# Batch 0 of an attention-and-routing kernel: eight rows of q ahead of v, key sums in two banks, the third range's query products amid the first quotient, and a 64-key remainder as 128 zero-padded rows

## The chip, the cores and the metric

The kernel runs on one core of one Trainium2 chip. The metric is the device time of one execution in microseconds (us). The engines are TensorE (PE in the profile; PEld is its weight load), VectorE (DVE), ScalarE (ACT), GpSimd (POOL) and SyncE (SP), which here only issues transfers.

## The reference

Two blocks in a row. The first is an attention without softmax, for 4 batches, 4 heads, 1088 positions and 32 values per head; the second sends its output through eight experts that are weighted by a Sinkhorn iteration.

```
phi(x) = outer product of S1 x and S2 x          # 8 x 8 = 64 features per position
kv  = sum over s of phi(k)[s] * v[s]             # 64 x 32 per head
z   = sum over s of phi(k)[s]                    # 64 per head
x   = (phi(q) . kv) / (phi(q) . z + 1e-6)        # 4352 rows of 128 (heads side by side)

P = exp(x w_gate - max);  8 times: rows to sum 1, columns to sum 1, times N / E
out = sum over e of P[:, e] * (relu(x w1[e]) w2[e])   # w1: 128 x 1024, w2: 1024 x 128
```

All arithmetic is in float32.

## The kernel before

**Layout.** Features and values lie on the 128 partitions, positions along the free axis. `xT` holds the attention's output as 128 x 4352. A batch has 1088 keys: eight tiles of 128 (`NT`) and a remainder of 64. PSUM has eight banks: four in a pool that is taken in turn through `bank()`, and four with the names s0 to s3 (`mps`).

**Keys.** `transpose_k` (L264, L266; DVE) turns the loaded keys into `kT`. `keys_ab` (L276, L281; TensorE, copied out by ACT in L279, L282) makes both projections, `keys_products` (L293; DVE) their outer products `kp` in three parts: tiles 0 to 3, tiles 4 to 7, and the remainder. `keys_sums` (L309; TensorE) multiplies `kp` with `v` and with ones, 72 matmuls over the nine tiles; those of the remainder use 64 rows of the array, the others 128. The sums of two heads lie in the lower, those of the other two in the upper 64 partitions of one bank. `keys_kept` (L324) copies both halves out: in batch 0 into `kvz`, one half by ACT, one by DVE; in the other batches both by ACT.

**Queries of batch 0.** They go in four ranges of columns, `fourths`: 0 to 256, 256 to 512, 512 to 800, 800 to 1088. For each: `transpose_q` (L259; DVE), `query_products` (L343; TensorE, in a 64-row, 128-column shape; ACT copies one factor out in L346), `multiply` (L351; DVE; the other factor is read from its bank), `fractions` (L360; TensorE: numerator and denominator into two banks) and `divide` (L371 to L378; DVE: transpose, add and reciprocal, transpose back, multiply into `xT`). The ranges from 512 on put one factor into `bank()` banks and the other into s2 and s3. The queries of the later batches take another way: `queries_ab` (L394, L397) writes their factors to memory (L401, L405), `repeat_a` and `repeat_b` (L411, L414) read them back repeated, `times` (L421; DVE) multiplies and `tops` (L430; TensorE) does the sums.

**Experts.** `steps()` is a generator of small steps of the expert products: `first` (L726, TensorE, and L728, ACT) makes four matmuls from `xT`, and eight steps later `into` (L788) adds the products of the second matrix into s0 to s3. Its first group are columns 0 to 512 of `xT`, in two halves of eight steps. Before each block of steps `sums_of_two` (L206; POOL, four sums) prepares an expert's weights.

**Order.** The order of TensorE and DVE is written out by hand in two `manual_schedule` blocks (that of ACT too in the first). `fill(n)` puts expert steps worth about n there; a step of the first group counts 0.57, and what is over or short is carried on. In the second block the order of ACT, POOL and SP follows from the program. Transfers are issued by SP in order: k, then q, v and the rest of q for batch 0, then the gate, the first weights, and q, k and v of the next batch.

The pool `aps` gives a bank anew only when all its readers are through, and a tile with one buffer is written again only when it has been read; engines wait for that through semaphores which the framework inserts.

Of the kernel before, what the change touches and what calls it, by code (L numbers as in the profile page):

```python
# [10 lines left out]
F32 = mybir.dt.float32  # L11
# [39 lines left out]
def kernel(  # L51
# [105 lines left out]
    for i in range(2):  # L157
        t = wk.tile([P, H + 1, NT + 1, D], F32, name=f"v{i}", bufs=1)
        nc.vector.memset(t[:, H], 1.0)
        v_slots.append(t)  # L160

# [25 lines left out]
    load_q(0, 0, 16)  # L187
    load_v(0)
    load_q(0, 16)
# [65 lines left out]
    keys, queries = {}, {}  # L255
# [12 lines left out]
    def keys_ab(b, parts=((0, NT),)):  # L268

        ab = wk.tile([P, 2, NT + 1, H * R], F32, tag="ab", name="ab", bufs=1)  # L270
        for lo, hi in parts:
            pk = bank()[:, 0:2 * H * R * (hi - lo)].rearrange("p (t n f) -> p t n f", t=hi - lo, n=2)
            for t in range(lo, hi):
                for s in range(2):
                    sl = slice(64 * s, 64 * (s + 1))
                    nc.tensor.matmul(pk[sl, t - lo].rearrange("p n f -> p (n f)"),  # L276
                                     kT[:, P * t + 64 * s:P * t + 64 * (s + 1)],
                                     wdf, start=True, stop=True, tile_position=(0, 64 * s))
            nc.scalar.copy(ab[:, :, lo:hi, :], pk.rearrange("p t n f -> p n t f"))  # L279
        pr = bank()[0:64, 0:2 * H * R]  # L280
        nc.tensor.matmul(pr, kT[:, NT * P:S], wdf, start=True, stop=True, tile_position=(0, 0))  # L281
        nc.scalar.copy(ab[0:64, :, NT, :], pr.rearrange("p (n f) -> p n f", n=2))  # L282
        keys[b] = ab

    def keys_products(b, part):
        ab = keys[b]
        if part == 0:
            products[b] = wk.tile([P, (NT + 1) * H, R, R], F32, tag="kp", name="kp", bufs=1)
        kp = products[b]
        lo, hi, n = ((0, NT // 2, P), (NT // 2, NT, P), (NT, NT + 1, 64))[part]  # L290
        g = (hi - lo) * H
        fa, fb = (ab[0:n, i, lo:hi, :].rearrange("p t (h r) -> p (t h) r", h=H) for i in range(2))
        nc.vector.tensor_tensor(kp[0:n, H * lo:H * hi], fa.unsqueeze(3).to_broadcast([n, g, R, R]),  # L293
                                fb.unsqueeze(2).to_broadcast([n, g, R, R]), op=Alu.mult)
# [3 lines left out]
    def keys_sums(b):  # L298

        kp, vx = products.pop(b), v_slots[b % 2]  # L300
        pv = bank()[:, 0:128].rearrange("p (i c d) -> p i c d", i=2, c=2)
# [3 lines left out]
        for t in range(NT + 1):  # L305
            n = P if t < NT else 64
            for h in range(H):
                i, s = divmod(h, 2)
                nc.tensor.matmul(pv[64 * s:64 * (s + 1), i], kp[0:n, H * t + h].rearrange("p i j -> p (i j)"),  # L309
                                 vx[0:n, slots[h], t, :], start=(t == 0 and i == 0), stop=(t == NT and i == 1),  # L310
                                 tile_position=(0, 64 * s))
# [4 lines left out]
    def keys_kept(b):  # L316
        pv = sums_of.pop(b)
        for s in range(2):
            sl = slice(64 * s, 64 * (s + 1))
            if b:  # L320
# [8 lines left out]
    def query_products(c):  # L329
# [7 lines left out]
        else:  # L337
            banks = [[(mps.tile([P, 512], F32, tag=f"s{2 + i}", name="s") if m else bank())[:, 0:n]
                      for m in range(2)] for i in range(2)]
# [1076 lines left out]
    with tc.manual_schedule(engines={engines.DVE, engines.PE, engines.Activation}):  # L1416
# [13 lines left out]
        transpose_q(0, fourths[0][1])  # L1430
        fractions(0, 1)
        fractions(0, 0)
        query_products(1)
        divide(0)
        transpose_q(1)
    with tc.manual_schedule(engines={engines.DVE, engines.PE}):
# [5 lines left out]
        for i in range(2):  # L1442
            multiply(1, i)
        fractions(1, 1)
        fractions(1, 0)
        query_products(2)
        divide(1)
        fill(1.7)
        for i in range(2):
            multiply(2, i)  # L1450
# [4 lines left out]
        fill(0.6)  # L1455
        divide(2)
        keys_ab(1)
        fill(0.6)
        query_products(3)
        keys_products(1, 0)  # L1460
        fill(0.75)
        for i in range(2):
            multiply(3, i)
        keys_products(1, 1)
        fill(1.5)
# [3 lines left out]
        fill(0.75)  # L1469
# [3 lines left out]
        fill(0.5)  # L1473
# [69 lines left out]
```

## Time and profile before

| | |
|---|---|
| median of 3 runs | 893.29 us (892.32 to 894.04) |
| profiled execution | 893.34 us, its span 891.6 us |
| granted clock of TensorE | 0.999 |
| TensorE busy | 882.3 us, 15316 matmuls |
| DVE busy | 764.5 us |
| ACT busy | 545.2 us |
| POOL busy | 276.0 us |
| DMA | 179.10 MB, mean 201 GB/s |

Times in the rows are microseconds from the start of the span. A row of the timeline gives start, length, engine, line, operation, output and inputs, shapes and count, and in brackets the idle time of the engine before it and what ended that. The chain of waits gives start, length, engine, tile and line. A row of the windows gives a stretch, its length, the busy time of PE, PEld, DVE, ACT and POOL with instruction counts, the granted clock, the share of the DMA engines' time and GB/s.

### The profile page before, as it was taken

The page shows a single profiled execution, that of the slowest core. Times are in us where ns is not written, and L with a number is a line of the kernel's source. Part 1 is how long each engine was busy: PE and PEld are TensorE (multiplying, and loading weights), DVE is VectorE, ACT ScalarE, POOL GpSimd, SP SyncE. Part 2 cuts the span into 40 slices and gives each one's busy share as a digit, 9 for nine tenths or more (in the row PEclk, how much of TensorE's full clock was granted, in tenths as well). Part 3 has the DMA queues.
Part 4 walks back from the last instruction along what each step waited for, and adds up shares of the span by engine and source line. Part 5 has one row for each costly group of instructions (what it writes and reads, how often), then busy time and mean ns, then how long its engine had stood idle before and what let it go on. Part 6 is the DMA issues. An engine that isn't in the chain of part 4 may idle for free.

```text
span 891.6 us, 36437 instructions
## 1 busy us (share of the span) xinstructions
PE 882.3 (99%) x15316; PEld 631.7 (71%) x15316; DVE 764.5 (86%) x1336; ACT 545.2 (61%) x1086; POOL 276.0 (31%) x313
## 2 busy tenths in 40 slices
PE   8999999999999999999999999999999999999997
PEld 5777544457667777777777777777877887877885
DVE  7679689888998888888888888888899899889986
ACT  3345456645666666666666666666666666666664
POOL 3121125464552223223213312322333222332311
PEclk9999999999999999999999999999999999999999
DMA  8999299786785876487667766765775875775871
GB/s 227 306 267 273 74 243 248 112 255 188 225 264 169 239 206 207 124 227 216 170 170 204 207 173 193 209 173 159 220 227 151 266 225 141 226 248 137 240 200 28
DMA packets 146419, 179.10 MB, mean 201 GB/s; under 512 B 55984, under 2 KB 93440, under 8 KB 145872
## 3 DMA queue, kind: packets, MB, share of 16 engines
q1 hardware_dynamic: 138624, 166.67, 65.1%
q0 software_dynamic: 6528, 9.95, 5.6%
q8 instruction: 121, 1.98, 0.9%
q14 instruction: 42, 0.34, 0.1%
q10 hardware_dynamic: 1104, 0.15, 0.1%
HBM read 134.22 MB, written 25.99 MB: 180 GB/s over the span
## 4 chain that ended last, share of the span: by engine, by line
PE 95%; DVE 2%; DMA 1%; ACT 1%; SPq 0%; issue 0%; POOLq 0%; POOL 0%; DVEq 0%
PE pair L1067 39%; PE s L1217 38%; PE a L726 8%; PE s L788 7%; PE a L309 1%; PE a L430 1%; DMA v<-in_v_dram 1%; DMA w<-z 0%; PE a L276 0%; PE a L394 0%; PE s L360 0%; DVE hb L741 0%; PE a L464 0%; PE a L343 0%; ACT hb L728 0%
## 5 line engine op out<-in xcount | busy, mean ns | idle before, releaser
L1067 PE MATMUL pair<-xf,w1x 64*64 64x256 f32 (+1 forms) x6736 | 497.4, 365 | 0.1
L1067 PEld LDWEIGHTS pair<-xf,w1x 64*64 64x64 f32 x6736 | 257.5, 133 | 91.5 <-DVE hb L1077 6.1
L1077 DVE TENSOR_TENSOR hb<-pair,copies 128x512 f32<-128x512 f32 (+1 forms) x354 | 233.8, 662 | 64.8 <-ACT xf L1090 25.0
L1217 PE MATMUL s<-hb,w 64*64 64x256 f32 (+1 forms) x3824 | 283.5, 365 | 0.0
L1217 PE MATMUL s<-hb,ws 64*64 64x256 f32 (+1 forms) x2848 | 211.5, 365 | 0.3 <-issue 0.3
L1080 ACT ACTIVATE hb<-hb 128x512 f32<-128x512 f32 (+1 forms) x238 | 144.4, 608 | 103.5 <-DVE hb L1077 98.3
L1217 PEld LDWEIGHTS s<-hb,w 64*64 64x64 f32 x3824 | 148.4, 133 | 47.9
L996 POOL TENSOR_TENSOR xf<-xT,pb 128x512 f32<-128x512 f32 (+1 forms) x60 | 74.5, 1243 | 257.7 <-ACT xf L1090 212.9
L1004 POOL TENSOR_TENSOR xf<-xf 128x512 f32<-128x512 f32 (+1 forms) x59 | 72.4, 1228 | 218.2 <-ACT xf L1090 144.2
L1217 PEld LDWEIGHTS s<-hb,ws 64*64 64x64 f32 x2848 | 110.6, 133 | 36.0 <-issue 0.7
L726 PE MATMUL a<-xT,w 128*64 128x416 f32 (+3 forms) x512 | 118.9, 466 | 0.8 <-DVE xT L378 0.8
L728 ACT ACTIVATE hb<-a 128x416 f32<-128x416 f32 (+3 forms) x128 | 59.6, 469 | 66.1 <-PE a L726 55.8
L1080 ACT ACTIVATE hb<-pair 128x512 f32<-128x512 f32 (+1 forms) x126 | 72.6, 576 | 44.5 <-PE pair L1067 44.5
L1124 DVE SCALAR_TENSOR_TENSOR hb<-hb 128x512 f32<-128x512 f32 (+1 forms) x118 | 80.4, 681 | 15.0 <-ACT hb L1080 2.9
L1154 ACT COPY copies<-pair 128x512 f32<-128x512 f32 (+1 forms) x118 | 66.5, 564 | 30.6 <-PE pair L1067 30.6
L1151 ACT COPY copies<-pair 128x512 f32<-128x512 f32 (+1 forms) x118 | 66.5, 564 | 29.7 <-PE pair L1067 29.7
L1147 ACT COPY copies<-pair 128x512 f32<-128x512 f32 (+1 forms) x118 | 66.6, 565 | 26.3 <-PE pair L1067 26.3
L1127 DVE TENSOR_TENSOR hb<-hb 128x512 f32<-128x512 f32 (+1 forms) x118 | 79.4, 673 | 2.8
L1128 DVE SCALAR_TENSOR_TENSOR hb<-hb 128x512 f32<-128x512 f32 (+1 forms) x118 | 80.6, 683 | 0.0
L1129 DVE TENSOR_TENSOR hb<-hb 128x512 f32<-128x512 f32 (+1 forms) x118 | 80.1, 679 | 0.0
L741 DVE TENSOR_TENSOR hb<-hb 128x416 f32<-128x416 f32 (+7 forms) x84 | 59.0, 703 | 15.0 <-ACT hb L728 7.2
L788 PE MATMUL s<-hb,ws 128*64 128x416 f32 (+3 forms) x224 | 71.1, 475 | 0.7 <-DVE hb L741 0.7
(188 smaller groups left out, 676.2 us busy)
## 6 DMA issues: line engine op xcount, KB each, us to landing
w1x<-w1x SPq DMA_DIRECT2D x135, 256.0 KB, 4.1
w<-w2x SPq DMA_DIRECT2D x103, 256.0 KB, 4.1
ws<-w2x SPq DMA_DIRECT2D x51, 256.0 KB, 3.4
pb<-pT SPq DMA_DIRECT2D x35, 256.0 KB, 4.3
xf<-xf SPq DMA_DIRECT2D x70, 128.0 KB, 2.8
ws<-w2x SPq DMA_DIRECT2D x52, 128.0 KB, 3.8
w1x<-w1x SPq DMA_DIRECT2D x7, 896.0 KB, 5.7
w1x<-w1x SPq DMA_DIRECT2D x45, 128.0 KB, 4.0
```

The source lines that it names most:

```text
L726: nc.tensor.matmul(ph[sl], loaded_w[j][0][:, P * f + H2 * s:P * f + H2 * (s + 1)], xT[:, at + lo:at + hi], start=True, stop=True, tile_pos ...
L788: nc.tensor.matmul(sums[g][i][H2 * s:H2 * (s + 1)], w, x, start=c == 1, stop=c == per, tile_position=(0, H2 * s))
L996: nc.gpsimd.tensor_tensor(xf[:, 0:2].rearrange("p b n -> p (b n)"), xT[:, lo:lo + 2 * n], weights.pop(i), op=Alu.mult)
L1004: nc.gpsimd.tensor_tensor(xf[:, 4:6], xf[:, 1:4:2], xf[:, 0:2], op=Alu.subtract)
L1067: nc.tensor.matmul(out[H2 * col:H2 * (col + 1), r], w1[rows, PLACE[form], o:o + H2], xf[rows, x], start=start, stop=stop, tile_position=(H ...
L1077: nc.vector.tensor_tensor(flat(out, n), x, flat(y, n), op=Alu.add)
L1080: nc.scalar.activation(out=x, in_=y, func=Act.Relu)
L1124: nc.vector.scalar_tensor_tensor(ts[:, 0], h[:, 3], 0.0, h[:, 0], op0=Alu.max, op1=Alu.subtract)
L1127: nc.vector.tensor_tensor(ts[:, 2], h[:, 1], ts[:, 0], op=Alu.subtract)
L1128: nc.vector.scalar_tensor_tensor(ts[:, 1], h[:, 3], 0.0, h[:, 1], op0=Alu.max, op1=Alu.subtract)
L1129: nc.vector.tensor_tensor(ts[:, 3], h[:, 2], ts[:, 2], op=Alu.subtract)
L1217: yield lambda rho=rho, rows=rows, c=c: nc.tensor.matmul(acc[g][rho][q][H2 * half:H2 * (half + 1), n * place:n * (place + 1)], w[rows], fl ...
```

## The change

- Batch 0's q is loaded in 8 and 26 rows (256 and 832 columns) around v, instead of 16 and 18.
- `ab` becomes one tile for all batches. Its rows 64 to 127 in the remainder's place, and those of both `v` tiles, are set to zero once by POOL; the third key product and the remainder's eight matmuls then cover 128 rows in every batch.
- In batch 0 the sums of the heads go to two banks, one for each half of the partitions.
- In the first block `transpose_q` covers ranges 1 and 2 only, and `query_products(2)` stands behind `query_products(1)`, ahead of `divide(0)`. Its second factor goes to s0 and s1 instead of s2 and s3.
- In the second block ranges 1 and 2 are multiplied one after the other, the fractions of both and the next keys follow, the last range of q is transposed ahead of `divide(1)`, and the fills are redistributed; they come to 8.0 before and after.

```diff
@@ -157,7 +157,11 @@
     for i in range(2):
         t = wk.tile([P, H + 1, NT + 1, D], F32, name=f"v{i}", bufs=1)
         nc.vector.memset(t[:, H], 1.0)
+        nc.gpsimd.memset(t[H2:P, 0:H, NT], 0.0)
         v_slots.append(t)
+
+    ab = wk.tile([P, 2, NT + 1, H * R], F32, name="ab", bufs=1)
+    nc.gpsimd.memset(ab[H2:P, :, NT], 0.0)
 
     loaded, pools = {}, []
 
@@ -184,9 +188,9 @@
                 in_=AP(tensor=v.tensor, offset=o + (4 * NT + c) * D, ap=[[SA * D, 32], [S * D, H], [1, D]]))
 
     load_k(0)
-    load_q(0, 0, 16)
+    load_q(0, 0, 8)
     load_v(0)
-    load_q(0, 16)
+    load_q(0, 8)
 
     def load_w(e, between=lambda: None):
         w1 = wpool.tile([P, F], F32, tag="w1", name="w1")
@@ -252,7 +256,7 @@
     load_v(1)
 
 
-    keys, queries = {}, {}
+    queries = {}
 
     def transpose_q(b, lo=0, hi=S):
         to = kT if b == 1 else qT
@@ -267,7 +271,6 @@
 
     def keys_ab(b, parts=((0, NT),)):
 
-        ab = wk.tile([P, 2, NT + 1, H * R], F32, tag="ab", name="ab", bufs=1)
         for lo, hi in parts:
             pk = bank()[:, 0:2 * H * R * (hi - lo)].rearrange("p (t n f) -> p t n f", t=hi - lo, n=2)
             for t in range(lo, hi):
@@ -280,43 +283,41 @@
         pr = bank()[0:64, 0:2 * H * R]
         nc.tensor.matmul(pr, kT[:, NT * P:S], wdf, start=True, stop=True, tile_position=(0, 0))
         nc.scalar.copy(ab[0:64, :, NT, :], pr.rearrange("p (n f) -> p n f", n=2))
-        keys[b] = ab
 
     def keys_products(b, part):
-        ab = keys[b]
         if part == 0:
             products[b] = wk.tile([P, (NT + 1) * H, R, R], F32, tag="kp", name="kp", bufs=1)
         kp = products[b]
-        lo, hi, n = ((0, NT // 2, P), (NT // 2, NT, P), (NT, NT + 1, 64))[part]
+        lo, hi = ((0, NT // 2), (NT // 2, NT), (NT, NT + 1))[part]
         g = (hi - lo) * H
-        fa, fb = (ab[0:n, i, lo:hi, :].rearrange("p t (h r) -> p (t h) r", h=H) for i in range(2))
-        nc.vector.tensor_tensor(kp[0:n, H * lo:H * hi], fa.unsqueeze(3).to_broadcast([n, g, R, R]),
-                                fb.unsqueeze(2).to_broadcast([n, g, R, R]), op=Alu.mult)
+        fa, fb = (ab[:, i, lo:hi, :].rearrange("p t (h r) -> p (t h) r", h=H) for i in range(2))
+        nc.vector.tensor_tensor(kp[:, H * lo:H * hi], fa.unsqueeze(3).to_broadcast([P, g, R, R]),
+                                fb.unsqueeze(2).to_broadcast([P, g, R, R]), op=Alu.mult)
 
     products = {}
 
     def keys_sums(b):
 
         kp, vx = products.pop(b), v_slots[b % 2]
-        pv = bank()[:, 0:128].rearrange("p (i c d) -> p i c d", i=2, c=2)
+        pv = [bank()[:, 0:128].rearrange("p (i c d) -> p i c d", i=2, c=2) for _ in range(1 if b else 2)]
 
         slots = [slice(h, H + 1, H - h) for h in range(H)]
 
         for t in range(NT + 1):
-            n = P if t < NT else 64
             for h in range(H):
                 i, s = divmod(h, 2)
-                nc.tensor.matmul(pv[64 * s:64 * (s + 1), i], kp[0:n, H * t + h].rearrange("p i j -> p (i j)"),
-                                 vx[0:n, slots[h], t, :], start=(t == 0 and i == 0), stop=(t == NT and i == 1),
-                                 tile_position=(0, 64 * s))
+                nc.tensor.matmul(pv[s % len(pv)][64 * s:64 * (s + 1), i],
+                                 kp[:, H * t + h].rearrange("p i j -> p (i j)"), vx[:, slots[h], t, :],
+                                 start=(t == 0 and i == 0), stop=(t == NT and i == 1), tile_position=(0, 64 * s))
         sums_of[b] = pv
 
     sums_of = {}
 
     def keys_kept(b):
-        pv = sums_of.pop(b)
+        pvs = sums_of.pop(b)
         for s in range(2):
             sl = slice(64 * s, 64 * (s + 1))
+            pv = pvs[s % len(pvs)]
             if b:
                 x, y = kvs[b % 2][sl, :, s, :], pv[sl].rearrange("p i c d -> p i (c d)")[:, :, 0:D + 1]
             else:
@@ -335,8 +336,8 @@
             pairs = [mps.tile([P, 512], F32, tag=f"s{2 * c + i}", name="s") for i in range(2)]
             banks = [[t[:, n * m:n * (m + 1)] for m in range(2)] for t in pairs]
         else:
-            banks = [[(mps.tile([P, 512], F32, tag=f"s{2 + i}", name="s") if m else bank())[:, 0:n]
-                      for m in range(2)] for i in range(2)]
+            banks = [[(mps.tile([P, 512], F32, tag=f"s{i if c == 2 else 2 + i}", name="s") if m else bank())
+                      [:, 0:n] for m in range(2)] for i in range(2)]
         for m in range(2):
             for i in range(2):
                 sl = slice(64 * i, 64 * (i + 1))
@@ -1427,10 +1428,11 @@
         for i in range(2):
             multiply(0, i)
         keys_kept(0)
-        transpose_q(0, fourths[0][1])
+        transpose_q(0, fourths[0][1], fourths[2][1])
         fractions(0, 1)
         fractions(0, 0)
         query_products(1)
+        query_products(2)
         divide(0)
         transpose_q(1)
     with tc.manual_schedule(engines={engines.DVE, engines.PE}):
@@ -1439,38 +1441,34 @@
         repeat_a(1)
         repeat_b(1)
         load_q(2)
-        for i in range(2):
-            multiply(1, i)
+        for c in (1, 2):
+            for i in range(2):
+                multiply(c, i)
         fractions(1, 1)
         fractions(1, 0)
-        query_products(2)
-        divide(1)
-        fill(1.7)
-        for i in range(2):
-            multiply(2, i)
         transpose_k(1)
         load_k(2)
         fractions(2, 1)
         fractions(2, 0)
-        fill(0.6)
+        transpose_q(0, fourths[2][1])
+        divide(1)
+        keys_ab(1)
         divide(2)
-        keys_ab(1)
-        fill(0.6)
+        fill(3)
         query_products(3)
         keys_products(1, 0)
-        fill(0.75)
         for i in range(2):
             multiply(3, i)
+        fill(0.9)
         keys_products(1, 1)
-        fill(1.5)
         fractions(3, 1)
         fractions(3, 0)
         keys_products(1, 2)
-        fill(0.75)
+        fill(1)
         divide(3)
         load_v(2)
         load_q(3)
-        fill(0.5)
+        fill(1.5)
         made = second_forms()
         for b in range(1, B):
             for i, n in enumerate(attention(b)):
```

## The prediction

> **What bounds the kernel now.** I read the page's first part and its chain, then the timeline of the first 38 us engine by engine, then the chain of waits in order of time.
>
> ```profile
> PE 882.3 (99%) x15316; PEld 631.7 (71%) x15316; DVE 764.5 (86%) x1336; ACT 545.2 (61%) x1086; POOL 276.0 (31%) x313
> ...
> PE 95%; DVE 2%; DMA 1%; ACT 1%; SPq 0%; issue 0%; POOLq 0%; POOL 0%; DVEq 0%
> ```
>
> TensorE is busy for 882.3 of 891.6 us and carries 95% of the chain: what TensorE does not have to do, or does not wait for, comes off the end. The change touches the first 30 us and the key sums of all four batches. This is the stage, by engine (start, length, engine, line, in brackets the idle time before and its releaser):
>
> ```profile
> 6.02 0.35 SPq L173 DMA_DIRECT2D qx<-in_q_dram  x1
> ...
> 7.38 0.40 DVE L259 STREAM_TRANSPOSE qT<-qx 128x256 f32<-128x256 f32 x1
> ...
> 7.93 2.69 DVE L293 TENSOR_TENSOR kp<-ab 128x1024 f32<-128x1024 f32 x3
> ...
> 9.65 2.46 PE L309 MATMUL a<-v,kp 128*64 128x64 f32 x72 [0.40 <-DMA v<-in_v_dram]
> ...
> 12.16 0.26 ACT L324 COPY kvz<-a 64x128 f32<-64x128 f32 x1 [2.23 <-PE a L309]
> 12.45 0.29 DVE L324 COPY kvz<-a 64x128 f32<-64x128 f32 x1 [1.17 <-ACT kvz L324]
> ...
> 12.78 1.04 DVE L259 STREAM_TRANSPOSE qT<-qx 128x832 f32<-128x832 f32 x1
> ...
> 12.80 1.08 PE L360 MATMUL a<-ph,kvz 128*64 128x256 f32 x8 [0.69 <-DVE kvz L324]
> 13.85 0.45 DVE L371 STREAM_TRANSPOSE rd<-a 128x256 f32<-128x256 f32 x1
> ...
> 13.88 1.13 PE L343 MATMUL s<-qT,wq 64*128 64x256 f32 x8
> ...
> 15.33 0.42 DVE L378 TENSOR_TENSOR xT<-a,rd 128x256 f32<-128x256 f32 x1
> ...
> 15.81 1.51 PE L726 MATMUL a<-xT,w 128*64 128x256 f32 x12 [0.80 <-DVE xT L378]
> ```
>
> TensorE stands idle three times: 0.40 us for v, 0.69 for the copies of the key sums (DVE's starts when ACT's has ended), 0.80 for the first quotient, whose transpose at 13.85 stands behind the 832-column transpose of q. That is 1.89 us, and after 15.81 the chain is nearly all TensorE:
>
> ```profile
> 4.25 5.27 DMA v<-in_v_dram
> 9.65 2.49 PE a L309 x72
> ...
> 17.32 0.99 PE a L394 x12
> ...
> 19.18 0.69 PE a L343 x4
> 19.86 0.48 PE s L343 x4
> 20.34 1.45 PE a L726 x12
> ...
> 23.19 0.93 PE a L276 x32
> ...
> 27.92 0.43 PE a L726 x4
> ...
> 32.34 2.24 PE a L309 x72
> 34.59 0.58 PE a L726 x4
> ```
>
> **Part 1: 64-key remainder as 128 rows.** 32 matmuls of 64 columns in the 128-row shape take 0.93 us (L276), 29 ns each, so 72 take 2.09. The second batch's key sums take 2.24, and the four matmuls behind them 0.58 instead of the usual 0.43. So the eight 64-row matmuls at the end cost 0.15 us going in and 0.15 coming out: 0.30 per batch, on the path, as the next matmul follows at once. With 128 rows there is one shape throughout. Batches 1 to 3: 3 x 0.30 = **-0.90 us** (the other two at the second's price; bounds 0 and 1.2). In batch 0 the 0.15 going in counts below; the way out lies in the wait for the copies. DVE's third key product has as many columns as before and costs nothing more. The three extra memsets lie on POOL, which has 0% of the chain. The Trainium skill (TensorEngine Tiling (Array Packing), Theoretical Speedup) speaks against this part: a contract dimension of 64 or less is where packing gives up to 2x; by that rule the padding gives up half of 8 x 29 ns, 0.12 us per batch, an estimate. No row bears it out, since all eight matmuls use the same row half, so none runs beside another there.
>
> **Part 2: 8 rows of q ahead of v, two banks.** v's last transfer lands at 4.25 + 5.27 = 9.52. Eight rows less before it are 128 KB:
>
> ```profile
> 8.00:9.00 1.00, 1.00 (x14) 0.73 (x9) 1.00 (x1) 0.47 (x2) 0.00 (x0) 1.00 1.15 235
> ```
>
> At 235 GB/s (last column) that is 0.55 us earlier, from below 0. TensorE is free at 9.65 - 0.40 = 9.25, so 0.40 at most is used, and not all: the second half of the key products is ready only at about 10.3 (7.93 + 2.69, less the small third one's share by columns, 0.30), while the first 32 matmuls would be through at 9.25 + 0.93 = 10.18. From 10.35 the other 40 take 1.16, and the last one's end comes about 0.25 later (2.49 - 2.09 - 0.15): 11.76 instead of 12.14. Then both copies start together, DVE's 0.29 ends at 12.07, and the fractions (L360) start at 12.13 instead of 12.80.
>
> DVE now transposes 544 columns instead of 832: 0.40 at 256 and 1.04 at 832 make 0.72, so until 12.79. The quotient's transpose also needs the first half of L360, which takes 0.67 (18.13 to 18.80, below): 12.80. The quotient takes 13.85 to 15.75, 1.90, so it is ready at 14.70.
>
> **Part 3: third range's query products amid the first quotient.** TensorE: L360 at 12.13, the second range's products 1.08 later (as 12.80 to 13.88) at 13.21; eight matmuls of 288 columns take twice 0.48 = 0.96, of 256 columns 0.85: free at 14.06. The third range fills until 15.02, its shape ends with 0.15, and L726 starts at 15.17, the quotient being ready: **-0.64** against 15.81. Banks are free: s0 and s1 after the first range's multiply, the other two after the copies. The same eight matmuls go from their old place: 20.34 - 19.18 = 1.16 with the way in, and 1.45 - 3 x 0.43 = 0.16 behind them: **-1.32**.
>
> **Part 4: the price behind it.** Between 16.5 and 20.3 no expert step stands any more among the attention's steps.
>
> ```profile
> 15.67 1.30 DVE L259 STREAM_TRANSPOSE kT<-qx 128x1088 f32<-128x1088 f32 x1
> ...
> 18.13 1.05 PE L360 MATMUL s<-ph,kvz 128*64 128x256 f32 x8
> ...
> 18.80 0.45 DVE L371 STREAM_TRANSPOSE rd<-s 128x256 f32<-128x256 f32 x1 [1.20 <-PE s L360]
> ...
> 19.29 0.17 DVE L373 TENSOR_SCALAR rc<-rd 128x8 f32<-128x8 f32 x1
> ...
> 20.62 0.81 DVE L351 TENSOR_TENSOR ph<-ph,s 128x288 f32<-128x288 f32 x2
> ...
> 21.34 1.24 DVE L264 STREAM_TRANSPOSE kT<-kx 128x1024 f32<-128x1024 f32 x1
> ...
> 22.63 0.44 DVE L371 STREAM_TRANSPOSE rd<-s 128x288 f32<-128x288 f32 x1
> ...
> 23.09 0.74 POOL L206 TENSOR_TENSOR ws<-w,ws 128x256 f32<-128x256 f32 x1
> ...
> 23.11 0.75 DVE L373 TENSOR_SCALAR rc<-rd 128x9 f32<-128x9 f32 x1
> ...
> 24.60 0.96 PE L343 MATMUL a<-qT,wq 64*128 64x288 f32 x4
> ...
> 24.72 0.46 DVE L378 TENSOR_TENSOR xT<-s,rd 128x288 f32<-128x288 f32 x1
> ...
> 25.23 0.81 PE L343 MATMUL s<-qT,wq 64*128 64x288 f32 x4
> ```
>
> TensorE: three steps of 0.43 from 15.17 end at 16.46, L394 takes 0.99 (17.45), the two fractions 0.86 and 0.97 (by columns, from 0.43 per four of 256; 19.3), the keys 0.99 (20.3), five steps 2.15 (22.45), and the fourth range's products begin; their second half is due at 22.45 + 0.15 + 0.48 = 23.1. It writes banks that the third quotient reads to its end. DVE: 14.70, transpose 1.30, two multiplies 0.72 and 0.81 make 17.5, about when TensorE wants the first fraction; the key transpose waits for L394 to have read kT (17.65) and with its short remainder ends at 19.1, just ahead of TensorE; the last piece of q makes 19.5; the second quotient 1.90, 21.4; the third 22.63 to 25.18 = 2.55, or 1.97 without the 0.58 by which L373 was longer at 23.11, beside POOL's sum, than at 19.29: 23.4 to 23.95. The wait is 0.3 to 0.85; before it was 25.23 - 25.08 = 0.15. Both hit would add another 0.58. I take **+0.6**, near the upper row: POOL's four sums of 0.74 ended at 23.83, begin 0.7 earlier with the queries' transfers before them (L394 at 16.46, before at 17.32), and so lie at about 20.2 to 23.1, over the third quotient again. The Trainium skill (SBUF — State Buffer, Who interferes with whom) has it that such a DVE instruction and POOL exclude each other, the first to issue holding the ports; the trace's 0.75 against 0.17 agrees.
>
> What lies downstream and must not become late:
>
> ```profile
> 33.00 1.83 DVE L421 TENSOR_TENSOR ph<-ph,rb 128x768 f32<-128x768 f32 x2 [0.81 <-DMA rb<-qb]
> ...
> 37.21 0.87 PE L430 MATMUL a<-kvs,ph 128*64 128x66 f32 x24
> ```
>
> The second batch's query factors come through memory; L421's first half is done at 33.9, wanted at 37.21. TensorE will be 1.66 us early there (0.64 + 1.32 - 0.6 + 0.30), so it fits even if nothing comes sooner. The loads of q and k for the third batch stay behind those reads in SP's queue; they now need the last piece of q (19.5) and the key transpose (19.1), both done long before. Later,
>
> ```profile
> 170.00:180.00 10.00, 10.00 (x64) 4.89 (x62) 8.27 (x13) 8.07 (x17) 0.00 (x0) 1.00 0.33 60
> ```
>
> the DMA engines have a third of their time taken, so the transfers do not pace the change of stages.
>
> Sum: -0.64 - 1.32 + 0.6 - 0.90 = -2.26. The profiled execution took 893.34 (span 891.6, 1.7 around it), 0.05 over the median of 893.29: **891.0 us**.
>
> **The rivals.**
> *No wait in part 4.* POOL misses both quotients and TensorE is slightly later than worked out: term +0.6 gone, 890.4. For it: 0.3 of the wait is within my rounding. Against: the order of the two works out so in every row.
> *The copies stay serial* because both write kvz: L360 0.3 later, L726 too: 891.3. For it: the row names kvz as releaser. Against: the two write different partitions, and ACT's copy reads the same bank.
> *DVE becomes the bound.* From 14.70 to about 25.9 DVE has hardly a gap; each delay moves the second half of the fourth range's products one for one. If L373 is hit in both quotients (0.58 more) and a key product or multiply beside POOL loses as much again, 1.2 goes back: 892.2. By the skill's rule above any such instruction can be held for one whole POOL operation, 0.74 here; an estimate by that gives 892.5.
> *The rest of q comes late, slower than before.* It was issued at 6.02 and had landed by 12.78 at the latest, as DVE did not wait; when, no row shows. It grows from 18 to 26 rows. At the worst rate the rows allow, 26/18 of 6.76 us, it lands at 15.8: transpose until 16.5, both ranges' products and the way out until 18.5, L726 3.3 late: 894.3. It decides from a landing at 12.5; from 14.75 on the kernel is slower than before, and what stands behind it in the queue (the second batch's q and k) is later too. Against: 235 GB/s and a queue that serves v first make 10.5 likelier.
>
> **How the numbers follow.** 0.2% is 1.8 us, about what a measurement of this kernel can tell from no change. Forecast 0.49 (890.4 to 891.5), no wait 0.10, serial copies 0.05: faster by over 0.2%, 0.64. DVE bound 0.17, and 0.05 for a late q that lands by 16.5: within 0.2%, 0.22. Slower 0.14: 0.05 for a late q with what it delays behind it, 0.09 for another transfer or another order on ACT that no row names. The range 890.0 to 893.3 holds the first four, 0.81.
>
> **What would show it.** L309 in one shape only, 2.1 us from its start to the next line's in batches 1 to 3; both L324 copies at one time near 11.8; L343 as sixteen matmuls in one run from 13.2, then L726 at 15.2 with no idle time before it; a gap before the second half of the last L343 of 0.3 to 0.9 us. Wrong would be: DVE idle for q near 12; L726 not before 15.6; a wait of TensorE on kT; or L421 later than 34.

## The result, and the profile after

| | before | changed |
|---|---|---|
| median, first series (13 runs each) | 893.36 us (892.32 to 894.15) | 891.30 us (890.43 to 893.14) |
| median, second series (34 and 11 runs) | 893.85 us (892.92 to 895.36) | 892.91 us (891.85 to 894.73) |
| profiled execution, its span | 893.34, 891.6 us | 891.93, 890.1 us |

The ratio is 0.9979 (95% interval 0.9970 to 0.9987) in the first series, 2.06 us, and 0.9992 (0.9984 to 1.0001) in the second, 0.94 us. In the second the interval just takes in no change. So the change saves about two microseconds in one series and about one, not clear of noise, in the other, and the runs of the changed kernel lie further apart than those of the kernel before in both. The experiments find one transfer whose landing has a part in that; the larger part stays open.

The page's busy times and the engines' shares of the chain, the lines that answer to the first ones of the prediction:

```profile
PE 882.0 (99%) x15316; PEld 634.8 (71%) x15316; DVE 765.3 (86%) x1337; ACT 545.1 (61%) x1086; POOL 276.0 (31%) x316
...
PE 96%; DVE 2%; ACT 1%; DMA 1%; issue 0%; POOLq 0%; POOL 0%; DVEq 0%; SPq 0%
```

Little is seen there: TensorE is busy for 0.3 us less in a span 1.5 us shorter. The timeline of batch 0 shows it (lines are one to four higher than before: L309 is still the key sums, L325 their copies, L344 the query products, L361 the fractions, L727 the experts' first product, L422 and L431 the second batch's query factors and sums):

```profile
5.93 1.29 DVE L268 STREAM_TRANSPOSE kT<-kx 128x512 f32<-128x512 f32 x2
...
9.15 2.48 PE L309 MATMUL a<-v,kp 128*64 128x64 f32 x72
...
11.65 0.26 ACT L325 COPY kvz<-a 64x128 f32<-64x128 f32 x1 [1.84 <-PE a L309]
11.70 0.29 DVE L325 COPY kvz<-a 64x128 f32<-64x128 f32 x1 [0.52 <-PE a L309]
12.02 0.74 DVE L263 STREAM_TRANSPOSE qT<-qx 128x544 f32<-128x544 f32 x1
12.14 1.08 PE L361 MATMUL a<-ph,kvz 128*64 128x256 f32 x8 [0.51 <-DVE kvz L325]
...
13.15 1.13 PE L344 MATMUL s<-qT,wq 64*128 64x256 f32 x8
...
15.19 1.51 PE L727 MATMUL a<-xT,w 128*64 128x256 f32 x12
...
19.12 1.13 POOL L406 DMA_DIRECT2D qb<-qab  x2
...
19.82 0.42 DVE L374 TENSOR_SCALAR rc<-rd 128x8 f32<-128x8 f32 x1
20.22 0.78 POOL L210 TENSOR_TENSOR ws<-w 128x256 f32<-128x256 f32 x1
...
21.77 0.73 POOL L210 TENSOR_TENSOR ws<-w 128x256 f32<-128x256 f32 x1
21.91 0.62 DVE L374 TENSOR_SCALAR rc<-rd 128x9 f32<-128x9 f32 x1
...
22.64 0.76 PE L344 MATMUL a<-qT,wq 64*128 64x288 f32 x4
...
23.91 0.76 PE L344 MATMUL s<-qT,wq 64*128 64x288 f32 x4 [0.51 <-DVE xT L379]
...
34.55 1.83 DVE L422 TENSOR_TENSOR ph<-ph,rb 128x768 f32<-128x768 f32 x2 [5.17 <-DMA rb<-qb]
35.72 0.92 PE L431 MATMUL a<-kvs,ph 128*64 128x66 f32 x24
```

The wait for v is gone, both copies stand side by side, L727 follows the query products with no idle time, and two new things show: 0.51 us of TensorE ahead of the last query products, and DVE idle for 5.17 us until the repeated query factors `rb` have landed. The chain of waits at the key sums of batches 1 to 3 shows one shape:

```profile
30.96 2.10 PE a L309 x72
33.06 0.43 PE a L727 x4
...
58.60 2.16 PE a L309 x70
...
83.40 2.10 PE a L309 x72
```

Before they began at 32.34, 60.08 and 85.19: 1.38, 1.48 and 1.79 us are gained by then, and 2.08 at the next step after the last.

### The profile page after: what moved, and what is told of

Same layout as the page of the kernel before. It is cut to its first block, busy times and chain, and to the rows that moved or that the text cites. A ratio compares the mean times of both kernels' runs of the same rounds, so it can differ in the third digit from the quotient of the medians.

```text
span 890.1 us, 36449 instructions
## 1 busy us (share of the span) xinstructions
PE 882.0 (99%) x15316; PEld 634.8 (71%) x15316; DVE 765.3 (86%) x1337; ACT 545.1 (61%) x1086; POOL 276.0 (31%) x316
## 4 chain that ended last, share of the span: by engine, by line
PE 96%; DVE 2%; ACT 1%; DMA 1%; issue 0%; POOLq 0%; POOL 0%; DVEq 0%; SPq 0%
PE pair L1068 39%; PE s L1218 38%; PE a L727 8%; PE s L789 7%; PE a L309 1%; PE a L431 1%; PE a L279 0%; DMA w<-z 0%; PE s L344 0%; PE a L395 0%; PE s L361 0%; DVE hb L742 0%; PE a L465 0%; DMA raw<-in_S_dram 0%; ACT hb L729 0%
## 5 line engine op out<-in xcount | busy, mean ns | idle before, releaser
L1068 PEld LDWEIGHTS pair<-xf,w1x 64*64 64x64 f32 x6736 | 260.6, 133 | 90.7 <-DVE hb L1078 5.8
L1218 PE MATMUL s<-hb,ws 64*64 64x256 f32 (+1 forms) x2848 | 213.9, 365 | 0.3 <-issue 0.3
L1218 PEld LDWEIGHTS s<-hb,w 64*64 64x64 f32 x3824 | 150.9, 133 | 47.7
L1218 PEld LDWEIGHTS s<-hb,ws 64*64 64x64 f32 x2848 | 112.9, 133 | 35.8 <-issue 0.8
L727 PE MATMUL a<-xT,w 128*64 128x416 f32 (+3 forms) x512 | 118.9, 465 | 0.0
L742 DVE TENSOR_TENSOR hb<-hb 128x416 f32<-128x416 f32 (+7 forms) x84 | 59.1, 704 | 13.1 <-ACT hb L729 5.5
```

Source lines behind the costliest of these rows:

```text
L727: nc.tensor.matmul(ph[sl], loaded_w[j][0][:, P * f + H2 * s:P * f + H2 * (s + 1)], xT[:, at + lo:at + hi], start=True, stop=True, tile_pos ...
L1068: nc.tensor.matmul(out[H2 * col:H2 * (col + 1), r], w1[rows, PLACE[form], o:o + H2], xf[rows, x], start=start, stop=stop, tile_position=(H ...
L1218: yield lambda rho=rho, rows=rows, c=c: nc.tensor.matmul(acc[g][rho][q][H2 * half:H2 * (half + 1), n * place:n * (place + 1)], w[rows], fl ...
```

## The experiments

Where a time is compared between executions, it is counted from the first transpose of keys (L268), which starts at 5.93 to 6.40 as k lands. From there to the second batch's key sums it is 26.31 us in the kernel before (6.03 to 32.34) and 25.03 in the changed one (5.93 to 30.96): 1.28 of the 1.38 are the change's own, 0.10 an earlier k.

**e1, the padding alone**: the kernel before with only

```diff
-                nc.tensor.matmul(..., kp[0:n, ...], vx[0:n, ...], ...)   # n = 64 in the remainder
+                nc.tensor.matmul(..., kp[:, ...], vx[:, ...], ...)       # 128 rows, zero-padded
```

> The kernel before with the 128-row remainder alone (zeroed rows, one ab tile; old order, one bank, 16 rows of q first). Shape theory: the eight 64-row matmuls cost a change of shape going in and one coming out, 0.15 us each. So the key sums of batches 1 to 3 take 2.10 us from their start to the next line's instead of 2.24, the four expert matmuls behind them 0.43 to 0.48 instead of 0.58, and batch 0's sums end 0.15 sooner: -0.90 - 0.15, 892.3. Rival (a 64-row matmul is the cheaper one, so padding wastes half of it): the eight take as long or longer, 893.4 to 893.9.

892.53 us against 893.19, ratio 0.9991 (0.9982 to 1.0000); 26.09 us to the key sums of batch 1, 0.22 sooner. Those take 2.10 us and the next step 0.43, as the shape theory has it; of the 1.05 us expected in the whole 0.66 came.

**e2, the change without the padding**: `n = P if t < NT else H2` put back into the loop of `keys_sums`.

> The changed kernel with the remainder's eight matmuls in 64 rows again, all else as changed. Shape theory: key sums of batch 1 take 2.24 instead of 2.10, the four matmuls behind them 0.58 instead of 0.43, so +0.30 in each of batches 1 to 3 and +0.15 in batch 0: 892.3 to 892.4 where the changed kernel has 891.3. Rival (the padding did nothing, all came from the first 30 us): 891.3.

892.68 us, ratio 0.9994 (0.9985 to 1.0003). Its key sums of batch 1 began after 24.51 us, 0.52 sooner than in the changed kernel, which has the same work ahead of them but for one change of shape (0.15 us, see e3), so that 0.67 are to be explained. The timeline tells why:

```profile
20.01 0.17 DVE L375 TENSOR_SCALAR rc<-rd 128x8 f32<-128x8 f32 x1
...
21.27 0.73 POOL L210 TENSOR_TENSOR ws<-ws,w 128x256 f32<-128x256 f32 x1
...
21.85 0.19 DVE L375 TENSOR_SCALAR rc<-rd 128x9 f32<-128x9 f32 x1
21.96 0.73 POOL L210 TENSOR_TENSOR ws<-w 128x256 f32<-128x256 f32 x1
...
22.83 0.76 PE L345 MATMUL a<-qT,wq 64*128 64x288 f32 x4
...
23.42 0.75 PE L345 MATMUL s<-qT,wq 64*128 64x288 f32 x4
```

In this execution DVE's short steps (L375 here, L374 in the changed kernel) took 0.17 and 0.19 us, instead of 0.42 and 0.62: the first was over before POOL's first sum began (20.41), the second began 0.15 us before the end of the sum from 21.27. TensorE's wait at the fourth range is not there: the second half of its products starts 0.59 us after the first half (22.83 and 23.42), in the changed kernel 1.27 (22.64 and 23.91). The difference of 0.68 is what was to be explained. It is what the rival "no wait" described; and yet the whole time did not fall: in this profile 1.9 us go again at the landing of `rb` (table behind e12).

**e3, the remainder in two places**: as e2, with the eight 64-row matmuls in two groups of four, one after the fourth tile, one at the end.

```diff
+        order[4 * H:4 * H] = [(NT, 0), (NT, 1)]
+        order += [(NT, 2), (NT, 3)]
```

> As the run before it, but the eight 64-row matmuls of every batch stand in two groups of four, one after the fourth tile, one at the end: the same matmuls, twice as many changes of shape. Shape theory: 0.30 more per batch, so L309 of batch 1 takes 2.54 us to the next line's start where one group gives 2.24; in all +1.2 over the run before. Rival (the 64-row matmuls are slow by themselves, about 0.04 each): 2.24 as with one group.

893.51 us in one execution. The chain of waits in e2, and below it in e3, at the key sums of batch 1:

```profile
30.47 2.24 PE a L310 x72
32.71 0.58 PE a L728 x4
```

```profile
31.58 2.54 PE a L313 x72
34.12 0.58 PE a L731 x4
```

With 128 rows alone the sums take 2.10 and the next step 0.43. One group of 64-row matmuls makes 2.24 + 0.58, 0.29 more; two make 2.54 + 0.58, 0.59 more. The price is 0.15 us for each change of shape, not for the rows: eight matmuls in two places cost twice what they cost in one. The Trainium skill (TensorEngine Tiling (Array Packing), Key Properties) says that a change of the tiling mode drains TensorE; these rows agree and give the price.

**e4, one bank**: the changed kernel with both halves of batch 0's sums in one bank.

```diff
-        pv = [bank()... for _ in range(1 if b else 2)]
+        pv = [bank()... for _ in range(1)]
```

> The changed kernel with batch 0's key sums in one bank again. Bank theory: DVE's copy waits for ACT's, so it starts at 11.95 instead of 11.70, the fractions at 12.4 instead of 12.14, the first expert step at 15.45 instead of 15.19; about +0.25 in all. Rival (it is the common kvz tile that made them serial, and two banks changed nothing): the copies overlap as in the changed kernel, no difference.

892.82 us in one execution. Its timeline:

```profile
12.07 0.26 ACT L325 COPY kvz<-a 64x128 f32<-64x128 f32 x1 [1.85 <-PE a L309]
12.37 0.29 DVE L325 COPY kvz<-a 64x128 f32<-64x128 f32 x1 [0.78 <-ACT kvz L325]
...
12.71 0.44 PE L361 MATMUL a<-ph,kvz 128*64 128x256 f32 x2 [0.69 <-DVE kvz L325]
```

DVE's copy starts 0.30 after ACT's again, though both write the partitions of `kvz` that they wrote in the changed kernel. So it is the common bank that they read which makes one wait for the other, not the common `kvz`. Whether the chip needs this order or only the semaphores ask for it, the run does not tell. From the start of L309 to L361 it is 3.15 us (9.56 to 12.71) against 2.99 (9.15 to 12.14): 0.16 on TensorE, where 0.25 was expected.

**e5, all but the order** (the changed kernel with the two blocks' order of before), and **e6, the order alone** (the kernel before with the new order):

```diff
-        transpose_q(0, fourths[0][1], fourths[2][1])
+        transpose_q(0, fourths[0][1])
         fractions(0, 1)
         fractions(0, 0)
         query_products(1)
-        query_products(2)
         divide(0)
...
```

> The changed kernel with the third range's products and the order of the second block as before; padding, two banks and 8 rows of q stay. By the terms of the prediction: fractions at 12.14 and the quotient at 14.7 as in the changed kernel, the first expert step at 14.8 right behind it, TensorE idle 0.3 to 0.4 us ahead of it, and the third range's eight matmuls later at 1.16 + 0.16. So batch 1's key sums start at 31.3 (changed kernel 30.96, before 32.34), and in all 891.5 to 891.7: the order is worth only 0.3 to 0.4. Rival (the order is the main part): 892.3 or more.

> The kernel before with the new order alone (16 rows of q first, one bank, 64-row remainder). By the terms: key sums and fractions as before (12.80), the shorter transpose of q lets the quotient start at 13.5, the products of ranges 1 and 2 fill TensorE from 13.88 to 15.7, the first expert step starts at 15.85 with no idle time; then -1.32 and a wait of 0.5 in the fourth range instead of 0.15: batch 1's key sums at 31.4, in all -0.95, 892.3. Rival (the order brings nothing without the earlier start): 893.0 or more.

e5: 893.42 us against 893.67, ratio 0.9993 (0.9984 to 1.0001); 25.67 us to batch 1's key sums, 0.64 gained. e6: 893.76, ratio 0.9997 (0.9988 to 1.0005); 25.51, 0.80 gained. The two gains, 1.44 together, nearly make the change's 1.28. In e5 L727 still waits 0.77 for the first quotient: with the old order the 832-column transpose is back, which the expectation had overlooked. Neither shows in the whole time what it shows in the stage, nor what was expected of it (891.5 to 891.7 and 892.3) (for e5, see the last point on the prediction).

**e7, one expert step ahead of the wait**: `fill(3)` and `fill(0.9)` become `fill(3.6)` and `fill(0.3)`, which moves a step from behind the last query products into the 0.51 us ahead of their second half.

> The changed kernel with one expert step (four L727, four L789, 0.87 us) moved from behind the fourth range's products to ahead of them, so that it covers the wait for the third quotient. Wait theory: the second half of those products no longer waits 0.51 us, batch 1's key sums start 0.4 to 0.5 sooner than 30.96. If nothing else binds: 890.9. Rival (the second batch's query factors, read back from memory, bind TensorE at L431): the key sums start sooner, but L431 starts 0.25 us after the end of the first half of L422 as in the changed kernel (35.72 after 35.47), and the time stays at 891.3.

892.77 us against 893.67, ratio 0.9985 (0.9977 to 0.9994). The waits of TensorE in the stage, from 5 to 35 us:

```profile
PE a L361 <- DVE kvz L325: 0.5, 1, 0.5
PE s L361 <- DVE ph L352: 0.4, 1, 0.4
```

The wait at L344 is gone, and 0.4 us of it is back as a wait of the last fractions (L361) for DVE's multiply. The sums came at 24.90, 0.13 sooner, where 0.4 to 0.5 was expected.

**e8, more room ahead of L431**: two expert steps put ahead of batch 1's first query sums.

```diff
-        yield 1.7 if b == 1 else 2
+        yield 2.9 if b == 1 else 2
```

and 0.6 less in each of the two places behind.

> The changed kernel with two expert steps (1.7 us) moved from behind L431's second group to ahead of its first, so that TensorE wants the second batch's factors 1.7 us later; the same instructions otherwise. Factor theory (they landed at 34.5 in the changed kernel's profile, at 36.0 in two others, and TensorE then waited 0.9 to 1.7): no run waits there any more, L431 at about 37.4, the median falls to 890.8 to 891.1 and the high runs of the changed kernel (892.96, 893.14) go. Rival (the transfers bind nowhere in most runs): 891.3, same spread.

893.16 us (891.57 to 895.34), ratio 0.9989 (0.9980 to 0.9998); the expected 890.8 to 891.1 did not come. In its profiled execution, the longest (895.34), `rb` landed at 36.08 and L431 did not wait for it. But the two steps also stand ahead of the next batch's query products (L395 at 41.35 us, in the changed kernel at 39.37), whose trip through memory began later: its `rb` was issued at 54.73 instead of 50.24.

```profile
65.58 0.96 DVE L422 TENSOR_TENSOR ph<-ph,rb 128x768 f32<-128x768 f32 x1 [7.66 <-DMA rb<-qb]
...
66.64 0.92 PE L431 MATMUL a<-kvs,ph 128*64 128x66 f32 x24 [1.95 <-ACT qab L398]
```

The wait had moved to batch 2, where TensorE stood idle for 1.95 us in this execution.

**e9, POOL's weight sums away from the third quotient**: e7, with the four sums of L210 held until batch 1's sums are near, by one element that ACT writes into their tile in order, and their place in the program one block of steps later (the cut shows the first of the two).

```diff
+        if e == 0:
+            tc.keep_in_program_order(nc.scalar.copy(ws[:, 0, 0, 0:1], ones[:, 0:1]))
```

> The changed kernel with one expert step moved ahead (a step before the third range's second half instead of after it, as in e7) and GpSimd's four weight sums of expert 0 held back until batch 1's sums of keys are under way, so that they no longer stand beside the third range's quotient. Theory (the two quotient steps of L374 took 0.42 and 0.62 us because GpSimd's sums L210 ran beside them): both L374 take about 0.17 us, the third range's quotient ends 0.6 to 0.7 us sooner, neither the query sums nor the last range's fractions wait for VectorE, and batch 1's sums of keys start 24.3 to 24.6 us after batch 0's first transpose of keys (changed kernel 25.0, e7 24.9). Rival (the length of L374 has another cause): they stay at 0.4 to 0.6 us and the sums start where e7's did. For the whole time: if the landing of batch 1's repeated query factors still ends the wait ahead of L431, the time stays at the changed kernel's, 891 to 892; if nothing ends later, it falls by 0.5 us more.

892.19 us against 893.85, ratio 0.9985 (0.9976 to 0.9993). The timeline, and the waits from 5 to 35 us:

```profile
20.00 0.17 DVE L376 TENSOR_SCALAR rc<-rd 128x8 f32<-128x8 f32 x1
...
21.84 0.17 DVE L376 TENSOR_SCALAR rc<-rd 128x9 f32<-128x9 f32 x1
...
23.47 1.59 POOL L212 TENSOR_TENSOR ws<-w 128x256 f32<-128x256 f32 x1 [3.05 <-ACT ws L207]
```

```profile
PE a L363 <- DVE kvz L327: 0.5, 1, 0.5
PE s L363 <- DVE ph L354: 0.4, 1, 0.4
```

Without the sums both steps of the quotient take 0.17 us instead of 0.42 and 0.62, in e11 too. For the second step that shows POOL's sums as the cause: in all twelve profiles with the sums in their place it ends 0.02 to 0.04 us after the sum that began before it. For the first the way is open: in the changed kernel it ends (20.24) with POOL's transfer issue L406 (20.25), when the first sum has just begun (20.22), and in e2 it took 0.17 with the sums in place. But the key sums came at 24.99, not sooner than in e7, so half of the expectation fell. With the step moved ahead, the query products are no longer held by the quotient; the 0.4 us at the last fractions hang on their own chain (products, ACT's copy, DVE's multiply), which an earlier quotient does not shorten. The sums held back with the old fills, where the quotient does set the wait, were not tried; e2's execution shows what that is worth in the stage, 0.67 us.

**e10, the later loads held back; e11, e9 and e10 together; e12, the changed kernel once more.** e10 was to issue k and v of batch 2, q of batch 3 and the next expert's weights only behind `keys_kept(1)` (the cut shows the new place; the old calls go, and k's load waits for an element that ACT writes):

```diff
+        if b == 1:
+            load_k(2, True)
+            load_v(2)
+            load_q(3)
```

> The changed kernel with the loads of k for batch 2, of the next expert's weights, of v for batch 2 and of q for batch 3 issued only after batch 1's sums of keys are kept (about 33 us), so that after the repeated query factors rb (L415, issued near 26 us) only q of batch 2 follows until then. Theory (rb, wanted at about 35.7 us, shares the full DMA engines with the loads issued behind it, and in part of the executions lands after its use): rb lands 1 to 3 us sooner, L422 starts by 33.5 us, L431 starts without a wait, and the time falls by 0.3 to 0.7 us below the changed kernel's of the same series, with less spread. Rival (the queues serve rb in order, behind what was issued before it): rb lands where it did, 34 to 36 us, and the time does not fall. A second rival: the loads held back are now late themselves, with waits for k of batch 2 at about 45 us or for rb of batch 2 near 60 us, and the time rises.

> e9 and e10 together. Theory: batch 1's sums of keys start 0.5 to 0.7 us sooner than in the changed kernel and L431 does not wait, so the time is 0.8 to 1.3 us below the changed kernel's. Rival: one of the two does not hold, and the time is that of the other alone, or the held loads cost more than both bring.

> The changed kernel once more, beside the three others. Theory (the landing of rb differs from execution to execution): in a second profiled execution L422 starts anywhere from 33.5 to 36 us, and the moment by which batch 1's sums of keys start stays 25.0 us after batch 0's first transpose of keys within 0.2 us; the median is again 1.7 to 2.1 us below the kernel before. Rival (the landing is fixed by the order of issues): L422 starts at 34.5 us again, within 0.2 us.

Against 893.85 in the same series: e10 891.75 us, ratio 0.9975 (0.9966 to 0.9984); e11 892.26, 0.9981 (0.9972 to 0.9990); e12 892.91. The timelines of e12 and e11, below each other, and SyncE's issues from `rb` on in e10:

```profile
35.38 1.83 DVE L422 TENSOR_TENSOR ph<-ph,rb 128x768 f32<-128x768 f32 x2 [5.66 <-DMA rb<-qb]
...
36.55 0.92 PE L431 MATMUL a<-kvs,ph 128*64 128x66 f32 x24 [0.51 <-ACT hb L729]
```

```profile
36.50 1.83 DVE L426 TENSOR_TENSOR ph<-ph,rb 128x768 f32<-128x768 f32 x2 [5.84 <-DMA rb<-qb]
...
37.67 0.92 PE L435 MATMUL a<-kvs,ph 128*64 128x66 f32 x24 [1.74 <-issue]
```

```profile
27.72 0.44 SPq L417 DMA_DIRECT2D rb<-qb  x1
...
28.68 0.44 SPq L200 DMA_DIRECT2D w<-in_moe_w_dram  x1
29.16 0.57 SPq L202 DMA_DIRECT2D w<-in_moe_w_dram  x1
29.83 3.93 SPq L172 DMA_DIRECT2D kx<-in_k_dram  x1
```

The edit held back less than it was meant to. The two weight transfers (512 KB each) still follow `rb` (1152 KB), by 0.96 and 1.44 us, sooner than in the changed kernel (1.57 and 2.53), since another place of the program loads them once the old call is gone; e11 has them at 0.88 and 1.45. Only k (544 KB) and what stands behind it moved, and v waited in the changed kernel too (its first issue, from 29.91, lasts 4.79 us, 4.5 of them a wait for TensorE). In e11 `rb` landed latest of all, 10.2 us after its issue at 26.34, in e10 7.1 us after it. So k's load is not needed to make `rb` late; with the weights still in place, the theory that the loads behind `rb` hold it up was not put to the test and stays open. Neither e10's landing at 34.77 nor e11's key sums (after 24.84 us, 0.19 sooner) and wait at L431 are what was expected. Why e10 had the lowest median of its series is not explained: against e12, by resampling the runs of both, it is 1.2 us lower with an interval from 2.9 lower to 0.2 higher. In its profile the stage is even 0.69 us longer than in the changed kernel, 25.72 to the key sums: a step of the quotient took 1.22 us (last section), and TensorE waits 1.19 at the fourth range instead of 0.51.

e12 has the stage of the changed kernel again (25.05 us), and its median gains 0.94 us where 1.7 to 2.1 was expected. The changed kernel itself had `rb` at 34.55 once and at 35.38 the next time. Of these 0.83 us 0.72 were already in the issue (26.48 and 27.20; k had landed 0.32 later), the rest in the landing; so the rival, a fixed landing, holds from the issue on (8.1 and 8.2 us) and not for the clock time.

**What the landing of `rb` costs.** Where nothing waits, L431 starts 4.57 us after batch 1's key sums (e7: 30.85 and 35.42), and 1.17 after L422 where L422 holds it (34.55 and 35.72 above). So L422 is wanted 3.40 us after the key sums, 3.70 where the 64-row remainder adds its 0.30. All times in us, one profiled execution each:

| | key sums of batch 1 | `rb` issued | L422 starts | wanted | late by | key sums of batches 1 to 2, beyond 27.44 (64 rows: 27.74) |
|---|---|---|---|---|---|---|
| before | 32.34 | 26.51 | 33.00 | 36.04 | no | 0.00 |
| e6 | 31.70 | 27.20 | 34.95 | 35.40 | no | 0.00 |
| e2 | 30.47 | 27.59 | 36.07 | 34.17 | 1.90 | 1.91 |
| e5 | 31.85 | 27.15 | 35.17 | 35.25 | no | 0.00 |
| e7 | 30.85 | 26.76 | 33.90 | 34.25 | no | 0.00 |
| e9 | 30.94 | 26.05 | 33.24 | 34.34 | no | 0.00 |
| changed | 30.96 | 26.48 | 34.55 | 34.36 | 0.19 | 0.20 |
| e12 | 31.30 | 27.20 | 35.38 | 34.70 | 0.68 | 0.69 |
| e11 | 31.18 | 26.34 | 36.50 | 34.58 | 1.92 | 1.93 |

The last column is measured apart from the others (the start of batch 2's key sums less that of batch 1's) and agrees with the lateness within 0.01 us. In e4, which is not in the table, it does not: `rb` (36.00) is 1.06 late, but 2.16 are lost until batch 2's key sums. There a step of DVE (L742 at 51.19) lasts 3.23 us, in the changed kernel 0.76 (49.74), while POOL's sums run from 51.70 to 53.80, and TensorE waits 0.74 for DVE behind it. From issue to L422 it is 6.5 to 10.2 us; e7 and the changed kernel, which issue the same transfers in the same order, have 7.1 and 8.1. What sets this is open. The kernel before has `rb` 3.04 us early in its profile, and would wait for none of these landings but the two latest; the changed one wants it 1.68 us sooner, amid them. So e2, which gained most in the stage, lost 1.9 us again at L431.

## Why the prediction was right, and where it was thin

The forecast was 891.0 us, 2.3 less than before. The first series came to 891.30; the second, with 892.91, gained 0.94 only, less than the 0.2% that the text took for measurable. That the first series came within 0.3 us of the forecast is thus in part luck. The mechanism held in its steps.

- **Padding, -0.90 foreseen.** Each use costs 0.29 us with the 64 rows (e2, e3), 0.87 for three, and the profile shows -0.31 from batch 2 to batch 3 and -0.29 behind it. The estimate from the Trainium skill's rule of packing, 0.12 us lost per batch, is not borne out.
- **v and the banks.** Both copies were foreseen near 11.78 and came at 11.65 and 11.70, L361 at 12.13 and came at 12.14, k having landed 0.10 sooner. e4 gives the bank 0.16 us on TensorE.
- **Third range amid the quotient.** L727 was foreseen at 15.17 and started at 15.19: -0.62 where -0.64 was foreseen, 0.10 of it from k's earlier landing. The working of part 4 left out that the three L727 behind the products take 1.51, as before, and not 1.29, which the sum does not use. From L727 to the last query products it is 7.45 us (15.19 to 22.64) against 8.79 before (15.81 to 24.60): -1.34 where -1.32 was foreseen.
- **The wait behind, +0.6 foreseen.** By the idle time in brackets it is 0.51. But the row ahead of it lasts 0.76, while in e2, where nothing waits, the second half starts 0.59 after the first. From first to second half it is 1.27 in the changed kernel and was 0.63 before (24.60 to 25.23), so the price is +0.64; before, by this measure, there was a wait of 0.04 and not of 0.15. The quotient ended as forecast (23.86, within 23.4 to 23.95). With 0.06 less behind the second half the four make -1.38 at the key sums of batch 1, where -1.36 was foreseen; without k's earlier landing -1.28. Both steps beside POOL were lengthened, as the text allowed, by 0.25 and 0.45, and e2 shows that the wait goes where they are short.
- **The rival "DVE becomes the bound"** is true of the stage, at a smaller price: e7 and e9 free TensorE at one place and find DVE and ACT at the next. The serial copies and the late q did not occur: DVE went from the copy at 11.70 to q's transpose at 12.02 without a wait.
- **The step that was thin is the slack of `rb`.** "It fits even if nothing comes sooner" took the 33.00 of one execution for a fixed time. L421 (now L422) later than 34 was named as what would prove the forecast wrong, and it came at 34.55. The 3.04 us of room were used up by 1.68 of earlier work and 1.55 of later landing: 0.19 us lost in one execution of the changed kernel, 0.68 in another, 1.9 in e2 and e11. It was no term of the sum, and it belongs into the range.
- **The rest.** In the profile 2.07 us are gained when the router's logits begin (the row below; 110.21 and 2.22 us before), 1.5 at the end of the span. 0.35 go in the logits themselves, which in the other executions took 2.15 to 2.88 us. What sets that length is open. From the start of the logits to the end of the span the fourteen profiles take 780.4 (e4) to 783.5 us (e5), the kernel before 781.4, the changed kernel 782.0 and, in e12, 782.5. This spread, behind all that the change touches, is larger than what `rb` costs. e5 was 1.39 us ahead of the kernel before when its logits began and 0.7 behind it at the end. Of the 1.4 us between the two profiles of the changed kernel 0.32 are k's landing, 0.49 `rb` and 0.58 lie behind the start of the logits. What makes them is open.

```profile
108.14 2.57 PE L465 MATMUL a<-xT,wg 128*32 128x512 f32 x24
```


## What to carry to other kernels

A wait taken from one engine is worth what the next latest arrival leaves of it: list every transfer that lands just ahead of its use, and hold its slack against the spread of landings over several executions, not against the one in the profile. Read in the trace whether an experiment moved what it was to move before reading its outcome: e10 left two of the transfers where they were. A short group of matmuls in another array shape costs its two changes of shape, so padding it with zeros can be cheaper than computing less. Two engines that copy from one PSUM bank may be put one after the other; two banks let them start together.

## What the runs showed of the hardware

The DMA engines are full from 20 to 30 us in every one of these executions (shares of 0.93 to 1.01), yet moved 253 to 329 GB/s there, most in the kernel before and in e9 and least in e2. The windows view of e2, 20 to 30 us (share and GB/s are the last two columns), and below it that of the kernel before:

```profile
20.00:30.00 10.00, 10.00 (x106) 6.70 (x104) 8.11 (x19) 5.12 (x14) 3.30 (x5) 1.00 0.93 253
```

```profile
20.00:30.00 10.00, 10.00 (x112) 6.50 (x110) 8.20 (x16) 5.34 (x15) 3.75 (x6) 1.00 1.01 329
```

The kernels differ in what they issue by then; but e7 and the changed kernel, with the same transfers, moved 307 and 287. A full share says how long the packets took and not how much they carried.

DVE's short step of the quotient stretched beyond what the forecast had as its worst: 1.22 us instead of 0.17 in e10, where it began 0.40 before a sum of POOL and ended 0.04 after it.

```profile
19.60 1.13 POOL L408 DMA_DIRECT2D qb<-qab  x2
...
20.30 1.22 DVE L376 TENSOR_SCALAR rc<-rd 128x8 f32<-128x8 f32 x1
...
20.70 0.78 POOL L212 TENSOR_TENSOR ws<-w 128x256 f32<-128x256 f32 x1
```

The Trainium skill (SBUF — State Buffer, Who interferes with whom) has the first to issue hold the shared ports and the other fully blocked. The second step of the quotient agrees: e2's L375 at 21.85 began 0.15 ahead of the end of a sum (22.00) and took 0.19, that of the changed kernel at 21.91 began 0.14 behind the start of one (21.77) and took 0.62; both ended 0.03 to 0.04 after that sum. e10's row cannot be read so simply: its step began ahead of the sum, but POOL's transfer issue L408 (19.60 to 20.73) was then under way. In e2 and e9 the same step, begun equally 0.42 us before the end of that issue, took 0.17. What held it in e10 no run here tells. In e9 the sums, held back, met DVE's key products instead: the first sum took 1.59 us from 23.47, where it takes 0.78 in the changed kernel, beside a key product from 23.25 (1.22).
